# Blockwise-causal attention and a two-layer projection: longer ways to TensorE in the planner, another rule for the shared port, and a new table of priorities

## The chip, the core and the metric

The kernel runs on one core of a Trainium2 chip. Such a core has a matrix engine (TensorE, PE in the profile), a vector engine (VectorE, DVE), an activation engine (ScalarE, ACT), a general one (GpSimd, POOL) and SyncE (SP), from whose queue nearly all transfers between the chip's memory and the on-chip buffers are issued. Each engine takes its own list of instructions in order; they wait for one another by semaphores. TensorE writes into eight banks of an accumulation memory, from which ScalarE and VectorE read.

The metric is the device time of one execution in microseconds; less is better. The time before is the median of three runs.

## What is computed

Attention over 8 batches of 8 heads, 576 positions of 64 numbers, with a mask in blocks of 64 (a position sees its own block and the blocks before), and on its result, as 4608 rows of 512 numbers, two projections with an activation between them. All is fp32.

```python
scores = scale * np.matmul(q, k.transpose(0, 1, 3, 2))
mask = block_i >= block_j                      # block = position // 64
scores = np.where(mask, scores, -1000000000.0)
scores = scores - np.max(scores, axis=-1, keepdims=True)
attn = np.exp(scores)
attn = attn / (np.sum(attn, axis=-1, keepdims=True) + 1e-09)
out = np.matmul(attn, v)
...
x = np.ascontiguousarray(attn_out.transpose(0, 2, 1, 3)).reshape(B * S, H * D)
h = x @ w_in                                   # 512 -> 2048
g = np.maximum(h, 0.0) + alpha * np.minimum(h, 0.0)
return (g @ w_out).astype(np.float32)          # 2048 -> 512
```

## The kernel before

**Products in parts.** Most products are made from a rounded form of fp32 (fp32r in the rows). For that nearly every operand is split into a high part (a cast by ScalarE: gh, wa, X, w) and a low part (the difference, by GpSimd or VectorE: gl, xl), and a product is three: high by high, high by low, low by high. `split` (L552 the cast, L553 the difference) does this for most operands, `activate` (L677 to L686) for the activations of the first blocks. The weights come as 64-bit floats and are taken apart by `to_f32` (L529 to L546: one load, one step on ScalarE, five on VectorE, with two accumulation banks) before they are split.

**Stages.** (1) Attention goes by pairs of heads, 32 of them, and within a pair by tiles of 128 queries: scores (L1002 or L997, for the last 64 queries L1061 or L1067), maximum on VectorE (L1018, L1012, L1074), exponential on ScalarE (L1021, L1081), sum and reciprocal on VectorE (L1025, L1027), scaling on GpSimd (L1029, L1088), transposes on TensorE (L1037, L1094, L1103), copies of these to PTF and PT (L1112, L1114), and the product with the values (L1138). (2) Beside it, in chunks of 256 rows, the first 6 of the 16 blocks of the hidden dimension (`chunk_a`: L666 the first projection, L699 the second, L881 the partial result). They need nothing of the attention but its finished rows, and fill TensorE while the attention's chains run on the other engines. (3) When the attention is done, the other ten blocks follow in nine chunks of 512 rows, as five pairs of blocks by a scheme with seven products where plain 2 x 2 blocking has eight. `factors` loads 1 MB of x (xb) and makes the seven X. `pair1` makes the seven products of the first projection (L742, six multiplications of 128 x 256 each), which share three banks x, y, z. Between them ScalarE copies a bank (`keep`, L751) that a later product of the same pair adds onto; VectorE adds such a copy onto another bank (`onto`, L755) or to a sum (L773); `act` (L759 ScalarE, L760 VectorE) makes the activation c. `chunk2` makes the seven products of the second projection (L800), of which each runs over the five pairs, needs the high and low part of an activation (or of a sum of activations, L785) and 256 KB of weights w from memory (L793), and ends in L813 or L818, which put it onto the partial result.

**What sets the order.** Nothing in the code's order does. Each piece of work is entered by `op` with its engine, a cost in ns, what it reads and writes, the buffers that it claims and a priority (less is earlier). `SHIFTS` holds small numbers that are added to the priorities: the key is the priority itself, rounded. Then `Plan.schedule` plays the program through once, event by event: an engine that is free takes, of its pieces that are ready, the one with the least priority for which buffers are free. A piece is ready when what it depends on has ended, plus a way between the two engines from the table `LAT` (in ns). The order in which the pieces were taken is the order in which the instructions are issued, engine by engine. The reckoned times themselves go nowhere else: on the chip an instruction waits for its semaphores, be the reckoning right or wrong.

Two further rules touch the change. The planner lets VectorE and GpSimd share a port: it holds back any GpSimd piece, and any VectorE piece whose cost is of the kind `Port`, while the other one has it (`port`, the time until which it is taken). When both are free at the same moment, the engine with the lesser next priority is asked first. And TensorE's pieces cost more where the planner reckons with a slower clock (`clock`), from the columns streamed in the window before.

Of the kernel before, what the change touches and what calls it, by code (L numbers as in the profile page):

```python
# [142 lines left out]
class Plan:  # L143
# [45 lines left out]
    def schedule(self):  # L189
# [22 lines left out]
        for i in range(n):  # L212
            if not waits[i]:
                heapq.heappush(events, (0.0, 0, i))
        blocked = {}
        port = 0.0

        def wake(key):
            for x in blocked.pop(key, ()):
# [14 lines left out]
        while events:  # L234
            t = events[0][0]
# [12 lines left out]
            for engine in sorted(ready, key=lambda e: (e in ("DVE", "POOL"), ready[e][0] if ready[e] else (0, 0))):  # L248
# [16 lines left out]
                if chosen is None:  # L265
                    continue
# [1022 lines left out]
```

## Time and profile before

| what | value |
|---|---|
| median of 3 runs | 1094.94 us (1093.42 to 1095.65) |
| the profiled execution: device time | 1101.07 us |
| its span, first to last instruction | 1099.3 us |
| mean granted TensorE clock | 0.996 of full |
| DMA | 233.37 MB, mean 212 GB/s |
| of it through memory | 150.22 MB read, 37.49 MB written |

The profile is one execution, taken apart by instruction. Its page gives the busy time of each engine (weight loads of TensorE apart, as PEld); the trace answers the same for any stretch of time, what an engine waited for, and the instructions in order of time. Times in such rows are in us from the span's start. A row of a timeline has the start, the time until its last instruction ended, the engine, the line, the operation, what is written and read, the shape and the count, and in brackets the idle time before it with what ended it. Idle time under 0.15 us is not listed as a wait. A multiplication's end is modelled, so that products which follow each other closely look like one busy stretch, even where the starts are a little apart.

### The profile page before, as it was taken

To read this page: it belongs to the slowest core of one execution; us is meant where nothing else is said; L and a number is where in the kernel's file an instruction comes from. 1 tells how busy PE (TensorE), PEld (TensorE's weight loads), DVE (VectorE), ACT (ScalarE), POOL (GpSimd) and SP (SyncE) were. 2 spreads that over 40 slices of the span, in tenths; PEclk is the share of its full clock that TensorE was granted. 3 is DMA by queue.
4 is the path that set the end of the run, shared out by engine and by line. 5 is a ranking of instruction groups with operands and counts; after the bars stand their busy time and mean duration, and the time that the engine had idled before them with its cause. 6 is when DMAs were issued, how large, how long until landed. Compare 5 with 4: busy or idle time off the path is not lost. (4 is left out here: it accounts for less than half of the span.)

```text
span 1099.3 us, 24631 instructions
## 1 busy us (share of the span) xinstructions
PE 1076.1 (98%) x8158; PEld 971.6 (88%) x8158; DVE 754.4 (69%) x1703; ACT 702.4 (64%) x1969; POOL 711.9 (65%) x913
## 2 busy tenths in 40 slices
PE   7989999999999999999999999999999999999998
PEld 4667788888988889888889898999999999999998
DVE  7977675575576664756647778686776768586666
ACT  7878866676676676667655465656565656565553
POOL 4767657757667666576548866585767667675731
PEclk9999999999999999999999999999999999999999
DMA  6596885877568675866515365587877768686874
GB/s 199 187 273 194 241 253 146 245 207 228 151 197 258 192 212 182 233 210 193 143 48 202 102 221 182 176 277 217 271 229 255 256 223 286 200 297 195 298 254 156
DMA packets 139807, 233.37 MB, mean 212 GB/s; under 512 B 14880, under 2 KB 52256, under 8 KB 139680
## 3 DMA queue, kind: packets, MB, share of 16 engines
q1 hardware_dynamic: 138960, 231.15, 68.7%
q8 instruction: 65, 1.06, 0.4%
q10 hardware_dynamic: 720, 0.66, 0.2%
q14 instruction: 62, 0.51, 0.1%
HBM read 150.22 MB, written 37.49 MB: 171 GB/s over the span
## 5 line engine op out<-in xcount | busy, mean ns | idle before, releaser
L742 PE MATMUL bank<-X,w 128*128 128x256 f32 x1890 | 247.7, 286 | 1.7 <-ACT X L552 1.0
L742 PEld LDWEIGHTS bank<-X,w 128*128 128x128 f32 x1890 | 235.8, 190 | 3.9 <-ACT X L552 1.2
L800 PE MATMUL bank<-w,gh 128*128 128x256 f32 x1260 | 228.2, 281 | 1.8 <-ACT gh L552 1.7
L553 POOL TENSOR_TENSOR gl<-c,gh 128x256 fp32r<-128x256 f32 x177 | 153.7, 883 | 100.0 <-ACT gh L552 99.9
L1029 POOL TENSOR_SCALAR p<-p,ri 128x256 f32<-128x256 f32 (+3 forms) x256 | 138.0, 554 | 90.8 <-DVE ri L1027 53.8
L800 PEld LDWEIGHTS bank<-w,gh 128*128 128x128 f32 x1260 | 193.6, 189 | 2.6 <-ACT gh L552 2.6
L800 PE MATMUL bank<-w,gl 128*128 128x256 f32 x630 | 177.4, 282 | 1.6 <-POOL gl L553 1.6
L1021 ACT ACTIVATE p<-bank,nm 128x384 f32<-128x384 f32 (+3 forms) x256 | 134.3, 534 | 29.4 <-DVE nm L1018 15.3
L699 PE MATMUL bank<-wa,gh 128*128 128x512 f32 x432 | 139.1, 403 | 0.0
L666 PE MATMUL bank<-xh,wa 128*128 128x256 f32 x864 | 127.5, 286 | 2.4 <-ACT wa L552 1.5
L552 ACT CAST gh<-c 128x256 fp32r<-128x256 f32 x199 | 80.2, 407 | 64.1 <-PE bank L800 56.6
L800 PEld LDWEIGHTS bank<-w,gl 128*128 128x128 f32 x630 | 118.9, 189 | 2.4 <-POOL gl L553 2.4
L666 PEld LDWEIGHTS bank<-xh,wa 128*128 128x128 f32 x864 | 114.0, 191 | 6.9 <-ACT wa L552 1.7
L686 POOL TENSOR_TENSOR gl<-g,gh 128x256 fp32r<-128x256 f32 x108 | 83.6, 777 | 41.6 <-ACT gh L683 24.4
L1037 PE MATMUL bank<-ident,p 128*128 128x128 f32 x640 | 100.4, 281 | 6.7 <-POOL p L1029 5.9
L997 PE MATMUL bank<-K,Q 128*128 128x512 f32 (+1 forms) x448 | 93.9, 332 | 1.9 <-DMA K<-KL 1.2
L1138 PE MATMUL bank<-PTF,vraw 128*64 128x320 f32 (+3 forms) x768 | 94.8, 386 | 0.4 <-ACT p L1021 0.4
L1037 PEld LDWEIGHTS bank<-ident,p 128*128 128x128 f32 x640 | 75.0, 143 | 22.6 <-POOL p L1029 12.6
L679 DVE SCALAR_TENSOR_TENSOR g<-g,oal,bank 128x256 f32<-128x256 f32 x108 | 51.6, 478 | 62.4 <-ACT g L677 61.8
L1018 DVE TENSOR_REDUCE nm<-bank 128x1 f32<-128x512 f32 (+3 forms) x144 | 80.3, 586 | 17.4 <-PE bank L997 12.4
L553 POOL TENSOR_TENSOR gl<-raw,gh 128x256 fp32r<-128x256 f32 x74 | 64.5, 882 | 36.0 <-ACT gh L552 35.7
L751 ACT COPY g<-bank 128x256 f32<-128x256 f32 x135 | 50.1, 372 | 56.8 <-PE bank L742 56.7
(163 smaller groups left out, 2179.1 us busy)
## 6 DMA issues: line engine op xcount, KB each, us to landing
w<-wd SPq DMA_DIRECT2D x315, 256.0 KB, 4.3
Q<-QH SPq DMA_DIRECT2D x56, 256.0 KB, 3.8
K<-KH SPq DMA_DIRECT2D x112, 128.0 KB, 3.6
vraw<-in_v SPq DMA_DIRECT2D x32, 320.0 KB, 3.4
qraw<-in_q SPq DMA_DIRECT2D x30, 320.0 KB, 4.1
xd<-xT SPq DMA_DIRECT2D x8, 1152.0 KB, 7.2
part<-o SPq DMA_DIRECT2D x36, 256.0 KB, 3.0
xb<-xd SPq DMA_DIRECT2D x9, 1024.0 KB, 7.6
```

What stands on the lines that cost most here:

```text
L553: op(on, c_pool(n) if on == "POOL" else c_ss(n), lambda: (nc.gpsimd if on == "POOL" else nc.vector).tensor_tensor(out=lo(), in0=src(), in1 ...
L666: nc.tensor.matmul(hp()[:, :n], ww()[:, 0, cc * P:(cc + 1) * P], x()[:, cc, :n], start=(i == 0 and cc == 0), stop=(i == 2 and cc == NCC - 1))
L686: op("POOL", c_pool(CHA), lambda: nc.gpsimd.tensor_tensor(out=gl(), in0=g(), in1=gh().bitcast(F32), op=ALU.subtract), r=[g, gh], w=[gl], p ...
L699: nc.tensor.matmul(acc(), a()[:, ts], ww(), start=(first and i == 0), stop=(last and i == 2))
L742: nc.tensor.matmul(bank()[:, :CHA], W()[:, i, 256 * at + P * c:256 * at + P * c + P], B()[:, j, CHA * c:CHA * c + CHA], start=(first and n ...
L800: nc.tensor.matmul(bank()[:, CHA * i:CHA * i + CHA], a()[:, P * i:P * i + P], W()[:, x], start=(first and g + i + n == 0), stop=(g == NG - ...
L997: nc.tensor.matmul(o, Q()[:, i, qs], K()[:, 2 * h + i, :w], start=(i == 0), stop=(i == 1))
L1018: op("DVE", c_dve(w), lambda h=h: nc.vector.tensor_reduce(out=nm()[:, h:h + 1], in_=sb[h]()[:, off[h]:off[h] + w], axis=AX.X, op=ALU.max, ...
L1021: op("ACT", 238 + w / 1.2, lambda h=h, t=t: nc.scalar.activation(out=t()[:, :w], in_=sb[h]()[:, off[h]:off[h] + w], func=AF.Exp, bias=nm() ...
L1029: op("POOL", 244 + w / 1.2, lambda h=h: nc.gpsimd.tensor_scalar(out=pts[h]()[:, :w], in0=pts[h]()[:, :w], scalar1=ri()[:, h:h + 1], scalar ...
L1037: nc.tensor.transpose(out=tp()[:, base + c * P:base + (c + 1) * P], in_=pts[h]()[:, c * P:(c + 1) * P], identity=ident)
L1138: nc.tensor.matmul(ob()[rows[h], a - q0:q1 - q0], V()[:, c, h, :], moving, start=(c == 0), stop=(c == cs[-1][0]))
```

## The change

Three edits, all in the planner. The pieces of work, their costs and buffers and what they depend on are the same: 7430 pieces before and after.

First, the ways from ScalarE, VectorE and GpSimd to TensorE are reckoned as 255, 235 and 220 ns instead of 158, 135 and 118. Second, an engine of the two on the port notes the time since when it has been held back by it (`since`), and where both could go, the one that has waited longer is asked first. Third, `SHIFTS` has other numbers and many more: it reaches the priorities of 4094 pieces in another way than before. Of the table one line stands here.

```diff
-    -11: 1.5, -6: -0.5, -4.5: 1.3, -4: -3, -3.5: -6.1, 0: 2.2, 0.5: 0.1, 1: 2.7, 2: 3.4, 4.5: -1.2, 9: 2.6, 10: 1.7, 10.5: -0.8, 11: -0.8,
+    -11.75: -0.1, -11.5: 0.3, -10.5: -0.6, -9: 2.6, -8: -0.8, -7: 0.9, -5.5: -6.8, -4.5: 1.1, -4: -1.8, -3.5: -6.1, -3: 6.4, 0: 2.6,
...
-LAT = {("PE", "ACT"): 200, ("PE", "DVE"): 200, ("PE", "POOL"): 250, ("PE", "SP"): 250, ("ACT", "DVE"): 140, ("ACT", "PE"): 158,
-       ("ACT", "POOL"): 178, ("ACT", "ACT"): 110, ("ACT", "SP"): 180, ("DVE", "ACT"): 120, ("DVE", "PE"): 135, ("DVE", "POOL"): 235,
-       ("DVE", "DVE"): 115, ("DVE", "SP"): 150, ("POOL", "ACT"): 90, ("POOL", "DVE"): 90, ("POOL", "PE"): 118, ("POOL", "POOL"): 60,
+LAT = {("PE", "ACT"): 200, ("PE", "DVE"): 200, ("PE", "POOL"): 250, ("PE", "SP"): 250, ("ACT", "DVE"): 140, ("ACT", "PE"): 255,
+       ("ACT", "POOL"): 178, ("ACT", "ACT"): 110, ("ACT", "SP"): 180, ("DVE", "ACT"): 120, ("DVE", "PE"): 235, ("DVE", "POOL"): 235,
+       ("DVE", "DVE"): 115, ("DVE", "SP"): 150, ("POOL", "ACT"): 90, ("POOL", "DVE"): 90, ("POOL", "PE"): 220, ("POOL", "POOL"): 60,
...
-        port = 0.0
+        port, since = 0.0, {}
...
-            for engine in sorted(ready, key=lambda e: (e in ("DVE", "POOL"), ready[e][0] if ready[e] else (0, 0))):
+            for engine in sorted(ready, key=lambda e: (e in ("DVE", "POOL"), since.get(e, t), ready[e][0] if ready[e] else (0, 0))):
...
                 if chosen is None:
+                    if held:
+                        since.setdefault(engine, t)
                     continue
+                since.pop(engine, None)
```

What the planner makes of it is another order. Because the table is longer, a line of the kernel from the planner's end on has a number that is 73 higher after the change (L742 is L815, L800 is L873, L552 is L625, L785 is L858). Three places follow.

TensorE in stage 3, near 699 us of the profile before. First what stood there: five products of one pair of blocks at L742 without a break, of which the third and the fifth write the bank of the first (bank_144), with one product in between each time.

```order
L800 MATMUL bank_191<-w_7280,gl_552 128x256
L742 MATMUL bank_144<-X_7444,w_7272 128x256 x6
L742 MATMUL bank_183<-X_6662,w_7272 128x256 x6
L742 MATMUL bank_144<-X_6674,w_7272 128x256 x6
L742 MATMUL bank_174<-X_7247,w_7272 128x256 x6
L742 MATMUL bank_144<-X_6705,w_7272 128x256 x6
L800 MATMUL bank_191<-w_7292,gh_617 128x256 x2
```

And what stands there now, for the same pair of blocks (weights w_7272; its first bank is bank_181).

```order
L815 MATMUL bank_181<-X_7418,w_7272 128x256 x6
L815 MATMUL bank_144<-X_6668,w_7272 128x256 x6
L815 MATMUL bank_234<-X_7247,w_7272 128x256 x6
L815 MATMUL bank_181<-X_6675,w_7272 128x256 x6
L873 MATMUL bank_183<-w_7292,gh_676 128x256 x2
L873 MATMUL bank_183<-w_7292,gl_680 128x256
L873 MATMUL bank_183<-w_7292,gh_676 128x256 x2
L873 MATMUL bank_183<-w_7292,gl_680 128x256
L815 MATMUL bank_174<-X_7418,w_7267 128x256 x6
L815 MATMUL bank_181<-X_6719,w_7272 128x256 x6
```

The product that re-uses the first bank comes after two others, its next re-use after a product of the second projection and one of the next pair of blocks (w_7267).

ScalarE at the end of the first chunk of stage 3, near 677 us of the profile before. First the order before: gh are the high parts for the second projection, X_7251 the cast of a factor from a newly loaded xb.

```order
L552 CAST gh_695<-o_1264 128x256
L552 CAST X_7251<-xb_6596 128x512
L552 CAST gh_883<-c_7338 128x256
L552 CAST gh_990<-c_7405 128x256
L552 CAST gh_1179<-c_7493 128x256
L552 CAST gh_543<-c_7572 128x256
L552 CAST gh_617<-o_1264 128x256
L552 CAST gh_695<-c_7353 128x256
```

And now, from the same high part of o on.

```order
L625 CAST gh_761<-o_1216 128x256
L625 CAST gh_821<-c_7328 128x256
L625 CAST gh_973<-c_7416 128x256
L625 CAST gh_1117<-c_7505 128x256
L832 ACTIVATE g_6730<-bank_172 128x256
L625 CAST gh_588<-c_7577 128x256
L625 CAST gh_676<-o_1216 128x256
L625 CAST gh_761<-c_7338 128x256
L625 CAST gh_821<-c_7524 128x256
L625 CAST X_7251<-xb_6601 128x512
```

The cast of X has moved behind seven casts of gh that stood behind it.

ScalarE in the attention's start, near 70 us of the profile before: wa_948 is the high part of the fifth block's weights for the first projection, the p are exponentials of one pair's score tiles, m_252 the weights on their way through `to_f32`.

```order
L1021 ACTIVATE p_211,s_132<-bank_193,nm_203 128x512
L1021 ACTIVATE p_218,s_132<-bank_181,nm_203 128x512
L1021 ACTIVATE p_222,s_134<-bank_172,nm_209 128x384
L1021 ACTIVATE p_231,s_134<-bank_183,nm_209 128x384
L534 ACTIVATE bank_172<-m_252,ebias 128x512
L534 ACTIVATE bank_183<-m_327,ebias 128x512
L1142 COPY xT<-bank_193 128x320
L1021 ACTIVATE p_198,s_136<-bank_234,nm_261 128x256
L1021 ACTIVATE p_206,s_136<-bank_234,nm_261 128x256
L1114 COPY PT_108<-bank_191 64x128
L552 CAST wa_948<-m_252 128x512
```

Now the same weights (wa_880) come through before the exponentials p_211 and p_218 of that pair.

```order
L607 ACTIVATE bank_181<-m_252,ebias 128x512
L1187 COPY PTF_107<-bank_183 128x4x128
L1154 ACTIVATE pl_394,s_140<-bank_174,nm_261 128x288
L1154 ACTIVATE pl_394,s_140<-bank_193,nm_261 128x288
L1187 COPY PTF_107<-bank_191 128x4x128
L972 ACTIVATE QH_690<-qraw_200 128x640
L625 CAST wa_880<-m_252 128x512
L977 CAST KH_697<-kraw_189 128x576
L1094 ACTIVATE p_211,s_132<-bank_183,nm_203 128x512
```

The cast of the weights and the step of `to_f32` ahead of it (L534 before, L607 now) have moved past that pair's four large exponentials.

156 rows, old and new, of the table SHIFTS are left out of this document.

## The prediction

> **What bounds the kernel now.** I read the page's busy times first, then the same by stage, then what TensorE waited for, then the order of the instructions in time at the places where it waited.
>
> ```profile
> span 1099.3 us, 24631 instructions
> ...
> PE 1076.1 (98%) x8158; PEld 971.6 (88%) x8158; DVE 754.4 (69%) x1703; ACT 702.4 (64%) x1969; POOL 711.9 (65%) x913
> ```
>
> TensorE is busy for 98% of the span and no other engine for more than 69%. The change removes no instruction, so only two things can move the time: idle time of TensorE and the pace of its products. The busy time by stretches says where they are (two answers; the second number is the stretch's length, then busy time and count for PE, weight loads, DVE, ACT, POOL, then the granted clock):
>
> ```profile
> 20.00:60.00 40.00, 37.99 (x264) 25.28 (x266) 36.82 (x95) 33.07 (x92) 29.14 (x38) 1.00 0.61 185
> 60.00:100.00 40.00, 36.30 (x239) 28.63 (x238) 32.28 (x82) 32.56 (x93) 25.41 (x31) 0.96 0.81 234
> 100.00:141.00 41.00, 38.77 (x300) 32.34 (x301) 25.20 (x76) 34.99 (x112) 27.80 (x40) 1.00 0.89 244
> ```
>
> ```profile
> 300.00:400.00 100.00, 100.00 (x725) 84.93 (x723) 67.89 (x176) 71.04 (x216) 67.11 (x91) 1.00 0.75 210
> ...
> 600.00:660.00 60.00, 58.35 (x412) 54.10 (x411) 44.73 (x80) 35.53 (x87) 45.82 (x50) 1.00 0.48 159
> 660.00:700.00 40.00, 37.43 (x287) 35.82 (x286) 30.15 (x58) 21.76 (x60) 26.45 (x31) 0.96 0.53 169
> 700.00:800.00 100.00, 100.00 (x835) 99.71 (x835) 71.93 (x136) 58.12 (x153) 67.13 (x80) 1.00 0.77 246
> ```
>
> Four regimes follow. From 20 to 141 us TensorE idles 2.01 + 3.70 + 2.23 = 7.94 us while ScalarE works 33.07, 32.56 and 34.99 us of each stretch and VectorE 36.82 of the first 40: there the helpers nearly set the pace. In the middle (300 to 400) nothing idles. From 600 to 700 two seams cost 1.65 and 2.57 us. From 700 on the page shows a full TensorE; what is lost there can only be pace.
>
> **Part 1, the first projection's steady stage (640 to 1066 us).** The waiting that the page cannot show is in the starts of the products:
>
> ```profile
> 699.34 3.87 PE L742 MATMUL bank<-X,w 128*128 128x256 f32 x30
> 703.05 0.28 PE L800 MATMUL bank<-w,gh 128*128 128x256 f32 x1
> ```
>
> ```profile
> 705.19 0.41 PE L800 MATMUL bank<-w,gh 128*128 128x256 f32 x2
> ...
> 708.00 0.28 PE L742 MATMUL bank<-X,w 128*128 128x256 f32 x1
> ```
>
> ```profile
> 700.31 0.38 ACT L751 COPY g<-bank 128x256 f32<-128x256 f32 x1 [0.43 <-PE bank L742]
> ```
>
> Thirty multiplications at L742 take 703.05 - 699.34 = 3.71 us, 123.7 ns each; the four L800 products from 705.19 to 708.00 are 24 of the same shape in 2.81 us, 117.1 ns each. The five L742 products lose 3.71 - 30 x 0.1171 = 0.20 us. The order shown for this place says why: the third and the fifth write a bank that the first and the third wrote, and ScalarE's copy (L751) must have read it in between. The first product's own 6 x 0.117 = 0.70 us end near 700.04; the copy runs from 700.31 to 700.69; the third product should start two products in, at 699.34 + 2 x 0.70 = 700.74. Only 50 ns are left for the signal from ScalarE to TensorE. The planner before allows 422 ns from the copy's start to the product (a cost of 264 and a way of 158); 380 of copying leave 42 of them for the way. After, it allows 519. So each such re-use loses up to 0.20 / 2 = 0.10 us.
>
> Counted over the whole order, 135 of L742's 315 products re-use a bank that ScalarE copies; in 117 of them one product lies between in the order before, and in 4 after, where 90 have two and nearly all others more. With one more product of 0.70 us in between the wait is gone. The price: at most 113 x 0.10 = 11.3 us, at least nothing, were the loss L742's own pace. A second bound comes from the whole stage:
>
> ```profile
> 700.00:1066.00 366.00, 366.00 (x3052) 364.92 (x3052) 261.48 (x488) 211.08 (x556) 241.64 (x289) 1.00 0.77 249
> ```
>
> It runs 366.00 / 3052 = 119.9 ns a multiplication; at 117.1 it would save 8.5 us there and 9.9 from 640 on. That takes all of L742's slowness for waiting, and the group above was a bad one, so I take half of its price, 0.05 us: 113 x 0.05 = **5.6 us** (0 to 9.9).
>
> **Part 2, the seam at 660 to 700 us.** The timeline there:
>
> ```profile
> 674.76 0.19 PEld L800 LDWEIGHTS bank<-w,gl 128*128 128x128 f32 x1 [0.51 <-POOL gl L553]
> ...
> 678.75 0.62 ACT L552 CAST X<-xb 128x512 fp32r<-128x512 f32 x1 [1.53 <-DMA xb<-xd]
> 679.28 1.32 ACT L552 CAST gh<-c 128x256 fp32r<-128x256 f32 x4
> ...
> 679.73 0.51 PE L800 MATMUL bank<-w,gh 128*128 128x256 f32 x2 [0.91 <-ACT gh L552]
> ```
>
> ScalarE stands at a cast of X for a 1 MB load that has not landed, and the casts that TensorE needs now (gh) are queued behind it: 0.91 us. Ahead of that TensorE waits for GpSimd's low parts. In the new order seven gh casts stand before that X cast, and VectorE's sums for the last two products (L785 before, L858 now) stand four to six places earlier. So I take the whole idle time, 2.57 us (low end 0.9, the gh wait alone). The clock adds to it:
>
> ```profile
> 678.10:681.50 3.40, 1.99 (x12) 1.58 (x13) 2.06 (x4) 2.51 (x8) 1.75 (x2) 1.00 0.91 306
> 681.50:684.90 3.40, 3.40 (x18) 3.40 (x18) 1.82 (x3) 1.11 (x3) 3.40 (x5) 0.50 0.75 248
> 684.90:688.30 3.40, 3.40 (x30) 3.40 (x29) 1.78 (x5) 1.73 (x5) 2.16 (x3) 1.00 0.08 14
> ```
>
> After a window in which TensorE worked 1.99 of 3.40 us its granted clock is 0.50 for the next 3.40 us: 18 multiplications instead of 30, a loss of 12 x 0.117 = 1.4 us. If the window is filled this goes too; I take half of it, 0.7, since a rest of the idle may be enough to keep it. Together **3.2 us** (0.9 to 4.0). The Trainium skill, "TensorE: Matmul & The Clock Gate", section "Part 1: The HAM clock gate", gives the half clock to at least one idle window of some 3.4 us; by that rule stalls of 1 us cause none, the dip would stay and this part would be 2.57. The trace disagrees here, since the window ahead of the dip was 1.99 us busy.
>
> **Part 3, the attention's start (20 to 141 us).** TensorE's longest waits there:
>
> ```profile
> PE bank L666 <- ACT wa L552: 1.5, 1, 1.5
> PE bank L1103 <- POOL pl L1088: 1.3, 1, 1.3
> PE bank L997 <- DMA K<-KL: 1.2, 1, 1.2
> PE bank L1037 <- POOL p L1029: 1.1, 1, 1.1
> PE bank L666 <- POOL wa L553: 0.8, 2, 0.6
> ```
>
> The first, and the 0.6 us in the last, are one event: the low and high parts of the fifth block's weights (wa), which ScalarE casts late. In the new order that cast (wa) stands ten places earlier on ScalarE and the products that use it only three earlier on TensorE, so 1.5 + 0.6 = 2.1 us go. For the other three the order gives no clear answer; with ScalarE at 85% here, what is put first makes something else late. I leave them at nothing, and charge **1.0 us** for fresh waits, as 1815 of the 2278 pieces into which the planner cuts TensorE's work change places; the bounds are that all of the 7.94 us goes, and that it doubles. Net **1.1 us** (from 5.8 worse, 2.1 - 7.9, to 7.9 better).
>
> **What stays.** Ahead of the first seam and in the tail the rows around the waits are the same in both orders:
>
> ```profile
> PE bank L742 <- ACT X L552: 1.0, 1, 1.0
> PE bank L742 <- ACT g L751: 0.6, 1, 0.6
> ```
>
> ```profile
> 1088.25 0.47 PE L800 MATMUL bank<-w,gh 128*128 128x256 f32 x2 [0.83 <-ACT gh L552]
> ```
>
> The 1.6 us of 600 to 660 and the 0.83 at 1088.25 stay, and so do the first 35 products of TensorE, to about 25 us. The rule on the port costs nothing on the chip: it is the planner's, and what it changes is the place of VectorE's and GpSimd's instructions, which is in the parts above. No DMA is added. At the second seam the load of xb stands behind two more weight loads of 256 KB; the X cast that it feeds has moved back further, which hides it.
>
> **Sum.** 5.6 + 3.2 + 1.1 = 9.9 us, taken as 10. The profiled execution took 1101.07 us, 1.77 more than its span; less 10 it would take 1091. The median of the runs, 1094.94, lies 6.1 below the profiled one, so **1084.9 us**.
>
> **Rivals.** (a) The early gain is given back: ScalarE's 33.07 of 40 us is the limit, so part 3 is nothing, the dip of the clock stays and part 1 is half: 2.8 + 2.6 = 5.4, 1089.5 us. (By the Trainium skill's rule above the dip stays in every case.) For it speaks that L742 may be slower than L800 by itself; against it, that the loss sits at the re-uses. (b) More goes: half of the 7.94 us early, 4.0 at the seam, 6 in the steady stage: 14, 1080.9 us. (c) The change does not do what it says: the 123.7 ns are L742's own pace, and of the rest only the 0.9 us of the gh wait is saved: about 1094. (d) Slower, by the weight loads of the second projection. The new order sets L800 products earlier and more evenly among L742, each needs its own 256 KB w, and in the stretch 678.10 to 681.50 the DMA share was already 0.91 at 306 GB/s. If a w came 1.5 us late twice in each of the nine chunks, that is 27 us against the 10 gained, 1112 us; it decides from about 0.6 us per wait. Against it: over 700 to 1066 the share is 0.77, and nothing waits for w there now.
>
> **How the numbers follow.** The forecast has a chance of 0.55, (a) 0.20, (b) 0.10, (c) 0.08, (d) 0.07. The range reaches from just under (b) to between (a) and (c), 1080 to 1092, and leaves out (c), (d) and the edge of (b); the doubled early waits alone, 6.9 us worse than I take them, still end inside it at 1091.8. A difference of 0.2%, 2.2 us, is about what a measurement of this kernel can tell from none. Faster by more than that are the forecast, (a) and (b), 0.85; within it is (c), 0.08; slower is (d), 0.07.
>
> **What would show it.** Part 1 is right if the stretch from 700 to 1066 holds a multiplication every 118.5 ns or less, and wrong if it still needs 119.9. Part 2 is right if the seam near 675 us has under 1 us of TensorE idle and no granted clock of 0.50 after it. Part 3 is right if ScalarE's wa no longer is among TensorE's waits and the idle time from 20 to 141 us is below 7 us. The whole is wrong if a wait for w, or one for X, shows up on TensorE after 640 us.

## The result, and the profile after

| kernel | median us (lowest to highest, runs) | before, in the same measurement | ratio, 95% interval |
|---|---|---|---|
| after | 1085.97 (1084.34 to 1293.82, 7) | 1095.08 (7 runs) | 0.9907 [0.9882, 0.9933] |
| after, measured again | 1086.57 (1085.19 to 1088.45, 4) | 1097.27 (29 runs) | 0.9902 [0.9888, 0.9917] |

The change makes the kernel 9 to 11 us faster; 1084.9 was predicted, 1080 to 1092 as the range. Single runs far above all others, like the one at 1293.82 us here, are left out of the ratios and of the figures below.

The page of after, span and busy times:

```profile
span 1083.5 us, 24603 instructions
...
PE 1065.6 (98%) x8158; PEld 967.9 (89%) x8158; DVE 758.6 (70%) x1703; ACT 699.6 (65%) x1969; POOL 710.9 (66%) x913
```

The share of TensorE is the same 98% with 15.8 us less span: a share says nothing here, only the stretches do. These are the stretches of after that answer to those of before (start and end, length, then busy time and count of PE, weight loads, DVE, ACT, POOL, granted clock, DMA share, GB/s):

```profile
20.00:60.00 40.00, 38.21 (x264) 25.12 (x261) 36.54 (x96) 34.51 (x97) 28.62 (x38) 1.00 0.62 189
60.00:100.00 40.00, 37.48 (x252) 31.18 (x251) 31.37 (x76) 31.76 (x87) 27.60 (x35) 0.96 0.86 244
100.00:141.00 41.00, 40.71 (x317) 33.72 (x317) 28.50 (x84) 35.55 (x116) 25.87 (x38) 1.00 0.85 233
```

```profile
600.00:660.00 60.00, 57.12 (x401) 52.80 (x400) 46.25 (x85) 36.07 (x91) 45.08 (x49) 1.00 0.45 148
700.00:800.00 100.00, 100.00 (x846) 99.98 (x845) 73.13 (x136) 59.51 (x156) 68.51 (x83) 1.00 0.79 255
700.00:1066.00 366.00, 366.00 (x3092) 365.98 (x3091) 271.86 (x507) 214.76 (x562) 241.53 (x288) 1.00 0.78 254
```

```profile
660.00:700.00 40.00, 39.97 (x332) 39.29 (x331) 32.91 (x61) 22.60 (x62) 27.02 (x32) 1.00 0.65 212
```

From 20 to 141 us TensorE idles 4.60 us where it idled 7.94. From 600 to 660 it idles 2.88, more than the 1.65 before. The second seam is full and its clock is 1.00: 332 multiplications where 287 stood. From 700 to 1066 there are 3092 multiplications for 3052, 118.4 ns each for 119.9.

What TensorE waited for, in the whole of after (line, who released it: us in total, times, longest; the five largest, of which the first and the fourth lie in the first 20 us, as they did before):

```profile
PE bank L1110 <- POOL p L1102: 4.3, 2, 2.8
PE bank L1140 <- DVE g L752: 2.2, 1, 2.2
PE bank L873 <- POOL gl L626: 1.2, 1, 1.2
PE bank L584 <- DVE warm L481: 1.1, 1, 1.1
PE bank L815 <- ACT X L625: 1.0, 1, 1.0
```

The 1.5 us for ScalarE's wa are gone. The 1.0 us for X at the first seam stayed. Two are new: 1.2 us for a low part gl at 638.33 us, and 2.2 us in the attention's start, with a window of half clock behind it. The timeline of after and its windows there:

```profile
63.87 0.40 PE L1140 MATMUL bank<-KH,QH 128*128 128x288 f32 x1 [2.22 <-DVE g L752]
```

```profile
61.82:65.24 3.42, 1.37 (x11) 1.37 (x12) 3.09 (x6) 0.79 (x2) 0.74 (x1) 1.00 0.76 204
65.24:68.65 3.41, 3.41 (x13) 2.84 (x12) 3.32 (x8) 3.00 (x8) 1.28 (x1) 0.50 0.67 214
```

### The profile page after: what moved, and what is told of

It is laid out like the page before. It is cut to its first block, busy times and chain, and to the rows that moved or that the text cites. A ratio compares the mean times of both kernels' runs of the same rounds, so it can differ in the third digit from the quotient of the medians.

```text
span 1083.5 us, 24603 instructions
## 1 busy us (share of the span) xinstructions
PE 1065.6 (98%) x8158; PEld 967.9 (89%) x8158; DVE 758.6 (70%) x1703; ACT 699.6 (65%) x1969; POOL 710.9 (66%) x913
## 4 chain that ended last, share of the span: by engine, by line
PE 93%; DVE 3%; ACT 1%; POOL 1%; DMA 1%; issue 1%; DVEq 0%; POOLq 0%; ACTq 0%
PE bank L873 21%; PE bank L815 20%; PE bank L739 14%; PE bank L772 14%; PE bank L1211 8%; PE bank L1070 6%; PE bank L1110 6%; PE bank L1140 2%; PE bank L1167 1%; DMA raw<-in_w_in 1%; DVE nm L1091 1%; PE bank L1075 0%; POOL w L626 0%; DVE bank L609 0%; ACT p L1094 0%
## 5 line engine op out<-in xcount | busy, mean ns | idle before, releaser
L815 PE MATMUL bank<-X,w 128*128 128x256 f32 x1890 | 245.5, 282 | 1.7 <-ACT X L625 1.0
L815 PEld LDWEIGHTS bank<-X,w 128*128 128x128 f32 x1890 | 233.3, 189 | 2.6 <-ACT X L625 1.2
L873 PE MATMUL bank<-w,gh 128*128 128x256 f32 x1260 | 229.4, 281 | 0.8 <-ACT gh L625 0.8
L873 PEld LDWEIGHTS bank<-w,gh 128*128 128x128 f32 x1260 | 193.8, 189 | 1.0 <-ACT gh L625 1.0
L873 PE MATMUL bank<-w,gl 128*128 128x256 f32 x630 | 177.7, 282 | 1.2 <-POOL gl L626 1.2
L1094 ACT ACTIVATE p<-bank,nm 128x256 f32<-128x256 f32 (+3 forms) x256 | 134.5, 539 | 32.4 <-DVE nm L1085 16.3
L873 PEld LDWEIGHTS bank<-w,gl 128*128 128x128 f32 x630 | 118.9, 189 | 2.1 <-POOL gl L626 2.0
L1110 PE MATMUL bank<-ident,p 128*128 128x128 f32 x640 | 97.7, 279 | 4.9 <-POOL p L1102 4.3
L625 ACT CAST gh<-c 128x256 fp32r<-128x256 f32 x195 | 78.6, 407 | 36.8 <-PE bank L873 32.4
L832 ACT ACTIVATE g<-bank 128x256 f32<-128x256 f32 x135 | 50.8, 384 | 67.9 <-DVE bank L828 58.5
L1070 PE MATMUL bank<-K,Q 128*128 128x512 f32 (+1 forms) x448 | 89.7, 327 | 0.3 <-ACT pl L1154 0.3
L772 PEld LDWEIGHTS bank<-wa,gh 128*128 128x128 f32 x432 | 75.7, 190 | 13.9 <-issue 0.9
```

The lines of the kernel that those rows point to most:

```text
L772: nc.tensor.matmul(acc(), a()[:, ts], ww(), start=(first and i == 0), stop=(last and i == 2))
L815: nc.tensor.matmul(bank()[:, :CHA], W()[:, i, 256 * at + P * c:256 * at + P * c + P], B()[:, j, CHA * c:CHA * c + CHA], start=(first and n ...
L873: nc.tensor.matmul(bank()[:, CHA * i:CHA * i + CHA], a()[:, P * i:P * i + P], W()[:, x], start=(first and g + i + n == 0), stop=(g == NG - ...
L1070: nc.tensor.matmul(o, Q()[:, i, qs], K()[:, 2 * h + i, :w], start=(i == 0), stop=(i == 1))
L1094: op("ACT", 238 + w / 1.2, lambda h=h, t=t: nc.scalar.activation(out=t()[:, :w], in_=sb[h]()[:, off[h]:off[h] + w], func=AF.Exp, bias=nm() ...
L1110: nc.tensor.transpose(out=tp()[:, base + c * P:base + (c + 1) * P], in_=pts[h]()[:, c * P:(c + 1) * P], identity=ident)
```

## A table of three times that carries the experiments

TensorE's work is 2278 pieces in every version, and in every order piece 1649 is the first product of stage 3. From there on all pieces are products of six multiplications of one shape. So three times divide every trace in the same way, whatever the order: when the attention ends (the start of piece 1649), how long both seams take (from there to the start of piece 1711, some 50 us later), and the steady stage (from there to the start of the last piece). With them stand how many of L742's 135 re-uses of a copied bank have just one product in between, in the order, and how many windows of half clock fell into the seams.

| kernel | before stage 3 | in stage 3 | attention ends at us | seams us | half clocks in them | steady us | re-uses |
|---|---|---|---|---|---|---|---|
| before | old | old | 632.49 | 53.19 | 1 | 409.06 | 117 |
| before_again | old | old | 629.17 | 50.69 | 0 | 409.12 | 117 |
| stage3_only | old | new table, new ways | 629.52 | 52.52 | 2 | 404.31 | 3 |
| stage3_ways | old | new ways | 626.80 | 54.14 | 2 | 403.91 | 3 |
| attention_only | new table, new ways | old | 627.32 | 50.20 | 0 | 409.99 | 117 |
| att_ways | new ways | old | 625.86 | 54.47 | 1 | 409.24 | 118 |
| att_table | new table | old | 630.71 | 51.08 | 0 | 409.26 | 116 |
| stage3_old_ways | new table, new ways | new table | 623.87 | 54.69 | 2 | 407.63 | 84 |
| after | new table, new ways | new table, new ways | 625.37 | 49.40 | 0 | 404.21 | 4 |
| after_again | the same | the same | 626.09 | 49.40 | 0 | 404.17 | 4 |
| ways_only | new ways | new ways | 624.67 | 49.82 | 0 | 403.92 | 5 |
| table_only | new table | new table | 631.65 | 50.96 | 0 | 407.92 | 82 |
| act_way | ScalarE's way | ScalarE's way | 635.33 | 50.11 | 0 | 403.93 | 5 |
| fifth_x | new table, new ways | the same, more room for X | 625.90 | 52.11 | 1 | 404.49 | 3 |

Each row is one execution. In the steady column the two executions of before, and the two of after, agree within 0.1 us. But attention_only, whose order in stage 3 is that of before on every engine, needs 0.9 us more, so a difference under 1 us says little there. The first column spreads by 5.7 us over four executions of one order (632.49, 629.17, 629.52, 626.80), so there only groups can be compared: these four end at 629.5 us on the mean, the seven with the three new ways before stage 3 between 623.87 and 627.32, at 625.6 on the mean, and the two with the new table alone at 630.71 and 631.65.

Of the re-uses counted in the last column those that lie in the steady stage itself are 108 where the whole count is 116 to 118, 74 of the 84, 73 of the 82, and none in the other rows. The others lie in the seams.

## First experiments: which half of the program

The halves were cut apart at the first piece of stage 3: a table and ways for the pieces before it, others from it on. For the ways that is this edit (here the new ways in stage 3 alone, stage3_ways; attention_only, att_ways and stage3_old_ways have the old ones in LAT3 and the new ones in LAT); for the table, only those entries were exchanged that reach the half in question.

```diff
+LAT3 = {("ACT", "PE"): 255, ("DVE", "PE"): 235, ("POOL", "PE"): 220}
...
-                    ready_at[j] = max(ready_at[j], end + lat + LAT.get((engine, self.ops[j][0]), 0))
+                    ready_at[j] = max(ready_at[j], end + lat + ((LAT3 if j >= self.stage3 else {}).get((engine, self.ops[j][0])) or LAT.get((engine, self.ops[j][0]), 0)))
...
+    plan.stage3 = len(plan.ops)
     cs = first(0)
```

The kernel before once more, for a second profile:

> The kernel before, profiled a second time, because its first profiled execution (1101.07 us) took 6 us more than the median of its runs. If the first was an odd execution, this one takes about 1095 us and reaches stage 3 (the 1649th piece of TensorE, 632.49 us in the first) some 5 us earlier, with the steady stage after 700 us as before (119.9 ns a multiplication). If profiling itself costs 6 us, it takes 1101 again and stage 3 begins near 632.

The new table and ways in stage 3 alone:

> The order of before up to the end of the attention; in stage 3 the new table and the longer ways. Theory A (stage 3 carries the gain, as predicted: 5.6 us by the re-used banks and 3.2 at the seam): 1095.1 - 8.8 = 1086.3 us, 1085 to 1088, and no wait of TensorE over 0.5 us at the seam near 675 us. Theory B (the attention carries 7 us of the profile's difference): 1092 to 1094 us.

The new table and ways until stage 3 alone:

> The other half: the new table, ways and port rule up to the end of the attention, stage 3 planned as before. Theory A: 1.1 us less than before, 1094 us, 1092.5 to 1095.5. Theory B: 1088 us, as the profile of after reaches stage 3 7.1 us earlier than that of before.

The new ways, not the table, in stage 3 alone:

> Before, with the longer ways in stage 3 alone and the old table. 3 of the 135 re-uses of a bank have one product between them instead of 117, and the cast of X still stands before the seven casts of gh. Theory A (a re-use with one product between costs 0.05 us): 114 x 0.05 = 5.7 us less, 1089.4 us, with the seam's idle time as before; the stretch after 700 us at 118.5 ns a multiplication or less. Rival (the pace is L742's own): 1095 us and 119.9 ns.

| kernel | median us (runs) | ratio to before, 95% interval |
|---|---|---|
| before_again | 1095.29 (1) | span 1093.5 us, where the first profile's was 1099.3 |
| stage3_only | 1092.73 (5) | 0.9961 [0.9947, 0.9976] |
| attention_only | 1093.74 (12) | 0.9968 [0.9958, 0.9978] |
| stage3_ways | 1094.76 (12) | 0.9968 [0.9954, 0.9981] |

The second profile of before, at 1095.29 us, shows that profiling does not cost the 6 us. Over the 82 runs of before that were measured beside the experiments the median is 1096.9 us, from 1092.8 to 1101.6: the first profile, 1101.07 us, was one of the slowest executions, and the second one of the faster ones.

Both halves give something, and neither gives all. No theory came as written: stage3_only lies 4.3 us below before, where A asked for 8.8 and for no wait over 0.5 us at the second seam (it has one of 1.5 us for gh); attention_only lies 3.5 us below, where A asked for 1.1 and B for 7. (The bare times lie in B's range for the one and in A's for the other, but before took 1097.8 us in this measurement, not 1095.1.) The steady stage is settled by these: 366 us of it hold this many multiplications in before_again, in stage3_only and in stage3_ways:

```profile
684.00:1050.00 366.00, 366.00 (x3054) 364.93 (x3053) 261.84 (x487) 211.16 (x557) 243.75 (x291) 1.00 0.77 247
```

```profile
684.00:1050.00 366.00, 366.00 (x3091) 365.98 (x3091) 266.36 (x491) 215.46 (x564) 245.40 (x293) 1.00 0.76 249
```

```profile
684.00:1050.00 366.00, 366.00 (x3094) 366.00 (x3094) 269.73 (x492) 216.39 (x565) 249.26 (x293) 1.00 0.78 251
```

The ways alone do it, 409.1 to 403.9 us. That stage3_ways is nevertheless only 0.32% faster, 3.5 us where 5.7 were expected, fits its seams: 54.14 us, with two windows of half clock around a wait of TensorE for ScalarE's gh. ScalarE itself had been idle before that cast, for a sum of VectorE's (L786) and not for a load (two answers, TensorE and ScalarE):

```profile
672.71 0.80 PE L801 MATMUL bank<-w,gh 128*128 128x256 f32 x2 [1.72 <-ACT gh L553]
```

```profile
672.25 0.41 ACT L553 CAST gh<-c 128x256 fp32r<-128x256 f32 x1 [2.87 <-DVE c L786]
```

And before_again shows what the prediction could not know: its second seam has neither the half clock nor the 0.91 us for gh, with the very same order. TensorE idles 1.66 us there instead of 2.57, nearly all of it in four waits for gl.

```profile
660.00:700.00 40.00, 38.34 (x307) 36.87 (x306) 30.76 (x58) 20.83 (x58) 27.85 (x34) 1.00 0.58 189
```

The cast of X waits for its load there too, but the load lands about 1 us earlier against the work (678.75 in the first profile, where TensorE is 3.4 us later at that place; 674.43 here), in a gap of ScalarE's:

```profile
674.43 0.62 ACT L552 CAST X<-xb 128x512 fp32r<-128x512 f32 x1 [0.57 <-DMA xb<-xd]
```

## Second experiments: ways or table, half by half

The changed kernel once more, after_again:

> The changed kernel once more, for a second profile and a second set of times. If its gain has the places read so far (steady stage about 4.9 us, attention's start about 3.5, the seam at 660 to 700 the rest), the stretch from 684 to 1050 us holds 3085 multiplications or more, the seam idles less than 1 us without a half clock after it, and the time is 8 to 11 us below that of the kernel before on the same chip. If the profile of after was a lucky execution, the seam shows idle time or a half clock again, and the time is 5 to 7 us below.

The new table everywhere, the new ways until stage 3:

> The changed kernel with the old ways to TensorE in stage 3 alone. In its order 84 of L742's 135 re-uses of a copied bank have one product in between, where before has 117 and after has 4. If each such re-use costs 0.05 us, it keeps 33 x 0.05 = 1.65 us of the steady stage's gain: about 3065 multiplications from 684 to 1050 us (before 3050 to 3054, after 3092), and the time is about 4 us above after, more if the seam is late again, since the cast of X stands ahead of the gh casts there as before. If the table alone sets the pace of L742, the stretch holds 3085 or more, and the time is within 2 us of after.

The old table, the new ways until stage 3:

> The kernel before with the longer ways until stage 3 begins, the old table and the old ways in stage 3. Both changed until stage 3 gave 3.5 us (attention_only). If the ways give it, this run is 3 to 4 us faster than before and idles less than 5 us from 20 to 141 us (5.2 to 7.9 in four executions with the old order, 4.2 and 4.6 with the new); if the table gives it, it is within 1 us of before and idles 5 to 8 us. From 684 us on it is as before in both cases (3045 to 3054 multiplications to 1050 us).

The new table until stage 3, the old ways:

> The kernel before with the new numbers of the table that act until stage 3, and the old ways throughout. If the table gives the early gain, 3 to 4 us faster than before and less than 5 us idle from 20 to 141 us; if the ways give it, within 1 us of before. If the two only work together, since the numbers were found with the new ways, both this run and the last stay within 1 us of before, or are slower.

| kernel | median us (runs) | ratio to before, 95% interval |
|---|---|---|
| stage3_old_ways | 1094.14 (12) | 0.9976 [0.9965, 0.9988] |
| att_ways | 1095.48 (11) | 0.9984 [0.9975, 0.9993] |
| att_table | 1098.81 (12) | 1.0020 [1.0006, 1.0034] |

after_again came as the first case of its expectation says: 1086.57 us (in the table of the result), 10.7 below before, with the second seam full as in after.

stage3_old_ways is the dose between: 84 re-uses instead of 117 or 4, and its stretch holds 3066 multiplications, where 3065 were expected.

```profile
684.00:1050.00 366.00, 366.00 (x3066) 365.14 (x3065) 263.74 (x489) 213.07 (x558) 239.25 (x290) 1.00 0.75 247
```

In the steady stage 108, 74 and no such re-uses stand beside 409.1, 407.6 and 404.2 us: (409.1 - 404.2) / 108 = 0.045 us for each, and 34 of them make 1.5 us, as measured. (The 0.043 us in an expectation below come of dividing by 113, with those in the seams.) Its time, 7.6 us above after where about 4 were expected, has the rest in the seams again: 54.69 us in the traced execution, 5.3 more than after.

In the attention the ways count too: by the groups above it ends 3.9 us earlier with them, and no earlier with the table alone. att_table is the one kernel here that is slower than before, by 0.2%. Neither of the two expectations for att_ways was right as a whole, though: it is 1.8 us faster, not 3 to 4. In the traced execution what the attention gained is lost at the second seam, in one wait and the half clock behind it (timeline, then windows, of att_ways):

```profile
673.55 0.50 PE L801 MATMUL bank<-w,gh 128*128 128x256 f32 x2 [2.38 <-ACT gh L553]
```

```profile
671.34:674.76 3.42, 0.62 (x3) 0.42 (x4) 3.42 (x7) 1.67 (x6) 1.36 (x3) 1.00 0.88 328
674.76:678.17 3.41, 3.41 (x17) 3.41 (x18) 2.28 (x4) 1.08 (x3) 3.41 (x5) 0.50 0.33 82
```

My theory then was: the ways give the attention's gain and the steady stage's, and the table is what keeps the seams full. The next runs took it apart.

## Third experiments: the ways alone, the table alone, and a try at the first seam

Of the change's three edits, ways_only has the one on the ways and nothing else:

```diff
...
-       ("ACT", "POOL"): 178, ("ACT", "ACT"): 110, ("ACT", "SP"): 180, ("DVE", "ACT"): 120, ("DVE", "PE"): 135, ("DVE", "POOL"): 235,
+       ("ACT", "POOL"): 178, ("ACT", "ACT"): 110, ("ACT", "SP"): 180, ("DVE", "ACT"): 120, ("DVE", "PE"): 235, ("DVE", "POOL"): 235,
...
```

> The kernel before with the longer ways everywhere and the old table. By the parts measured so far the ways give 3.6 us in the attention (att_ways) and 4.9 in the steady stage (5 re-uses with one product in between), 8.5 in all. If the table matters at the seam alone, the steady stretch holds 3085 multiplications or more, the stretch from the first product of stage 3 to the end of the second seam (TensorE's pieces 1648 to 1710) takes 51 us or more where after takes 49.4, with a half clock likely, and the time is 2 to 5 us above after, 5 to 9 below before. If the table is needed everywhere, the time is within 3 us of before. If it is not needed at all, within 1 us of after.

And table_only has the one on the table:

```diff
 SHIFTS = {
-    -11: 1.5, -6: -0.5, -4.5: 1.3, -4: -3, -3.5: -6.1, 0: 2.2, 0.5: 0.1, 1: 2.7, 2: 3.4, 4.5: -1.2, 9: 2.6, 10: 1.7, 10.5: -0.8, 11: -0.8,
+    -11.75: -0.1, -11.5: 0.3, -10.5: -0.6, -9: 2.6, -8: -0.8, -7: 0.9, -5.5: -6.8, -4.5: 1.1, -4: -1.8, -3.5: -6.1, -3: 6.4, 0: 2.6,
...
```

> The kernel before with the whole new table and the old ways. 82 re-uses with one product in between: at 0.043 us each the steady stage gains 35 x 0.043 = 1.5 us, about 3065 multiplications from 684 to 1050 us. The attention is as in att_table, 1 us slower than before. So within 2 us of before, if the parts add up; 4 us or more below it if the table carries a gain of its own at the seams.

The third had this edit on top of after:

```diff
-        rooms("wb", ("w1", 3, [2, 7 * 256], F32R), ("w2", 4, [2, 256], F32R), ("xb", 1, [NCC, CHB], F32), ("X", 4, [2, 512], F32R),
-              ("m", 2, [512], F32), ("ws", 1, [512], F32), ("xt", 2, [512], F32), ("g", 4, [CHA], F32), ("c", 12, [CHA], F32))
+        rooms("wb", ("w1", 3, [2, 7 * 256], F32R), ("w2", 4, [2, 256], F32R), ("xb", 1, [NCC, CHB], F32), ("X", 5, [2, 512], F32R),
+              ("m", 2, [512], F32), ("ws", 1, [512], F32), ("xt", 2, [512], F32), ("g", 4, [CHA], F32), ("c", 8, [CHA], F32))
...
-        rooms("fx", ("w1", 2, [2, 7 * 256], F32R), ("w2", W2N, [2, 256], F32R), ("X", 4, [2, 512], F32R), ("c", CN, [CHA], F32))
+        rooms("fx", ("w1", 2, [2, 7 * 256], F32R), ("w2", W2N, [2, 256], F32R), ("X", 3, [2, 512], F32R), ("c", CN + 4, [CHA], F32))
```

> The changed kernel with the memory of stage 3's beginning shared out otherwise: 5 instead of 4 buffers for X from the attention's end on, and 8 instead of 12 for c until the first blocks' memory is free, the rest of both after that. In the order only 57 of TensorE's pieces move, all from the first seam on. If the 1.03 us in which TensorE waits there for X is the fifth X's wait for memory, the idle time from 600 to 640 us falls from 2.88 to about 2.2 us or less, and the time is 0.5 to 1 us below after, too little for the times alone. If the wait only moves to the sixth X, the idle time stays between 2.6 and 3 us and the time as after's. If the second seam is disturbed, it idles over 1 us there and loses 2 us or more.

| kernel | median us (runs) | ratio to before, 95% interval |
|---|---|---|
| ways_only | 1085.16 (4) | 0.9879 [0.9865, 0.9892] |
| table_only | 1097.68 (11) | 1.0001 [0.9987, 1.0015] |
| fifth_x | 1088.94 (5) | 0.9914 [0.9900, 0.9927] |

**The theory on the table fell.** With the three ways and the old table the kernel is at least as fast as with all of the change (0.9879 beside 0.9902 and 0.9907; the intervals overlap, so not shown to be faster). Its second seam is full:

```profile
660.00:700.00 40.00, 39.70 (x334) 39.29 (x333) 29.77 (x56) 22.56 (x62) 28.54 (x35) 1.00 0.71 231
```

And the table without the ways is worth nothing that can be measured, as its expectation has it if the parts add up. The steady stage of the traced execution gains 1.2 us where 1.5 were reckoned, and its attention ends at 631.65 us, 2.2 later than the mean of the old order but within that order's spread.

fifth_x did what it was to do at the first seam and gained nothing by it. TensorE idles 1.12 us from 600 to 640 instead of 2.88, and the wait for X is gone; but in the second seam of the traced execution, full in after, ScalarE's gh comes late and a half clock follows. Nor is it shown to be slower than after: the intervals, 0.9900 to 0.9927 and 0.9888 to 0.9917, overlap.

```profile
600.00:640.00 40.00, 38.88 (x254) 35.17 (x253) 32.10 (x55) 22.52 (x53) 29.96 (x34) 1.00 0.52 178
660.00:700.00 40.00, 37.68 (x300) 36.96 (x299) 30.38 (x58) 20.75 (x55) 24.03 (x29) 0.96 0.60 192
```

```profile
670.01 0.51 PE L874 MATMUL bank<-w,gh 128*128 128x256 f32 x2 [1.75 <-ACT gh L626]
```

## Last experiment: one number

The planner itself shows that ScalarE's way decides the re-uses, and that it has a step: with 230 ns, and the other two ways as before, 114 re-uses have one product in between, with 240 there are 106, with 255 there are 5. It reckons 200 ns from TensorE to ScalarE and 264 for the copy; with 255 for the way back that is 719, and a product is reckoned as 712 (6 x 117.3 x 1.012). Just above it, a second product has to go in between.

```diff
-LAT = {("PE", "ACT"): 200, ("PE", "DVE"): 200, ("PE", "POOL"): 250, ("PE", "SP"): 250, ("ACT", "DVE"): 140, ("ACT", "PE"): 158,
+LAT = {("PE", "ACT"): 200, ("PE", "DVE"): 200, ("PE", "POOL"): 250, ("PE", "SP"): 250, ("ACT", "DVE"): 140, ("ACT", "PE"): 255,
```

> The kernel before with one number changed: the way from ScalarE to TensorE is reckoned as 255 ns instead of 158. In its order 5 re-uses of a bank have one product in between and 127 have two. If the steady stage needs this number alone, the stretch from 684 to 1050 us holds 3085 multiplications or more (4.9 us). In the attention the high parts come from ScalarE, but most waits on GpSimd, so the theory leaves 1 to 3 of the 3.6 us that the three ways together gave there. The seam is open: 49.4 to 54.7 us from the first product of stage 3 to the end of the second seam, with the seven orders so far. Together 1086 to 1091 us where before takes 1097, and as ways_only (12 us below before) if the one number does it all. If VectorE's and GpSimd's ways carry the gain, the stretch stays under 3060 and the time within 2 us of before.

It took 1094.37 us (12 runs), 0.9984 [0.9974, 0.9993], above the 1086 to 1091 that were expected. The steady stage has all of its gain, 403.93 us, and the seams are good, 50.11. But in the traced execution the attention ends at 635.3, 5.8 us later than the mean of the old order and 2.8 later than the latest of its four: the weights are late again, by more (waits of act_way from 20 to 155 us, and its busy times):

```profile
PE bank L699 <- ACT wa L552: 2.8, 1, 2.8
PE bank L1094 <- ACT p L1021: 1.3, 1, 1.3
...
PE bank L699 <- POOL wa L553: 0.9, 1, 0.9
```

```profile
60.00:100.00 40.00, 32.78 (x186) 25.56 (x185) 27.55 (x70) 26.87 (x75) 23.56 (x30) 0.83 0.75 216
```

A clock of 0.83 over 40 us is four windows of half clock (40 x 0.17 x 2 = 13.6 us, 3.41 each). So VectorE's and GpSimd's ways are not needed for the steady stage. In the attention the three ways together gain and ScalarE's alone does not; which of the other two is needed there, and by what waits, was not tested.

## Why the prediction was right, and which steps were not

The sum was 9.9 us. Against before_again (1095.29 us) the trace of after gives 629.17 - 625.37 = 3.8 in the attention, 50.69 - 49.40 = 1.3 at the seams and 409.12 - 404.21 = 4.9 in the steady stage: 10.0. Against the first profile, from which the terms had been read, the same places give 7.1, 3.8 and 4.9. So the total was right, but of its three terms only the first had its size. The second was taken 1.9 us too high and the third 2.7 too low, measured from before_again, and that these two nearly cancel was luck.

- **Part 1, the re-uses (5.6): right, mechanism and size.** From piece 1711 on 108 re-uses are gone and with them 4.9 us, 0.045 us each where 0.05 was taken; the other 5 lie in the seams, where they can't be told from the rest. stage3_ways and act_way, in which the steady stage has the old table and the three ways or ScalarE's alone, show 5.1 to 5.2 us; stage3_old_ways loses what the line gives (1.5 us), table_only a little less (1.2 for 1.6). Rival (c), L742 slow by itself, is out: between 700 and 1060 us its 251 products took 732 ns on the mean from start to next start before, and its 248 took 712 after, where L800's take 708 and 709. So L742's own slowness is 3 or 4 of those 24 ns, and the rest was waiting.
- **Part 2, the second seam (3.2): the rows came as predicted, the price holds for one execution only.** After has no idle time there, and no half clock. But of the 3.8 us that separate the first profile from after's at the seams, 2.5 belonged to that one execution: with the same order before_again needed 2.5 us less. The step that failed is "I take the whole idle time" together with the half clock: the 0.91 us for gh hung on a load's landing, which came about 1 us earlier against the work in the second execution, and without that wait no half clock followed. The new wait of 1.2 us at the first seam then took a part of the gain back. Nor is it the place of X's cast that settles it. att_table has five of the seven gh casts ahead of it, attention_only none of them, and the seams of both are free of half clocks; stage3_only has six ahead, and two half clocks. In the five other traces with a half clock at the second seam (stage3_only, stage3_ways, att_ways, stage3_old_ways, fifth_x) the late cast of gh does not stand behind a cast of X that waits for a load: ScalarE is idle just before it, 0.88 to 3.83 us, for a sum of VectorE's.
- **Part 3, the attention's start (1.1): too low.** The wa wait went, as predicted, and fresh waits came too: the 2.22 us at 63.87 in after, none above 1.2 us in after_again. The listed idle time from 20 to 141 us fell from 6.25 us in before_again to 4.60 and 4.32 in the two executions of after, by 1.7 and 1.9. The step that failed is that this idle time was taken for all there is to win: stage 3 begins 3.8 and 3.1 us earlier, so 2.1 and 1.2 us of the gain are not in it. Where these lie, in half clocks, in idle time after 141 us or in pauses too short to be listed, was not taken apart. Idle from 20 to 141 us being below 7 us, which I had named as the sign, is no sign: before_again has 6.25.
- **What stays: half right.** Both waits of the first seam and the 0.8 us of the tail stayed. A third came at the first seam, the 1.2 us for gl at 638.33: in after a product of L800 starts at 636.74 us, where before ran L742 alone from 637.82 to 645.20.
- **The port rule: wrong as told.** I wrote that it changes the places of VectorE's and GpSimd's instructions. It changes none: as the planner gives it, the kernel before with this rule alone has, on every engine, the order of before, and after without it the order of after.
- **The half clock.** The prediction set a rule of the Trainium skill ("TensorE: Matmul & The Clock Gate", section "Part 1: The HAM clock gate"), by which the dip would stay, beside a window that was 1.99 us busy; the runs side with the window (last section).
- **Rivals.** (d) did not come: nothing waits for w on TensorE, with the DMA share at 0.78. (a), which gave the early gain back and halved the steady one, and (b), with 14 us, did not come either.
- **The reference execution.** I added the terms on a profile of 1101 us and then went down by the 6.1 us to the median. That offset wasn't spread evenly: the two profiles of before differ by 3.3 us until stage 3 and 2.5 at the seams, the very places that two terms were read from.

What stays open: why some orders keep the seams full, and by which waits the three ways shorten the attention. The eight traces without a half clock at the seams need 49.4 to 51.1 us there, the six with one or two need 52.1 to 54.7; no count of the order that I tried tells them apart beforehand. At most there is a tendency: of the six traces in which the cast of X stands ahead of all seven gh casts, as in before, four have a half clock at the second seam, of the eight with four to seven of them ahead of it two.

How often an order falls into a half clock can be read for the whole kernel, not for the seams: every run has its mean granted clock, and (1 - clock) x 2 x time is an estimate of the time at half clock, to about 1 us in a single run. It is 6.3 us a run over 82 runs of before and 2.6 over ten of after. Of the others ways_only and attention_only have 3.8, table_only and att_table 4.8, att_ways 6.2, stage3_only 7.4, stage3_old_ways 10.8, act_way 11.7 and stage3_ways 13.3. So after has less half clock than before on the mean of its runs; by the same estimate that is worth at most half of the 3.7 us between them, 1.9 us. fifth_x, with 2.2 us over five runs, has no more of it than after, so the half clock of its trace is not typical.

## What to carry to other kernels

Where a scheduler reckons with a latency, look for the step that it decides (here: does copy and way fit under one product or not), and take the time from the starts of the instructions, not from the busy share. Before a large table is blamed or praised, run the small edits alone: three numbers gave at least as much as all of this change. And take a second profile before terms are read from waits that hang on a transfer.

## What had not been expected of the hardware

The granted clock is set for windows of 3.41 us, and a half clock needs no idle window. In each of the 14 traces the stretches at half clock begin on one grid of 3.41 us and, ahead of the tail, last one or two of its steps. From 18 us on the traces hold some 4300 windows of that grid at full clock. All ten in which TensorE was busy for less than 0.53 of the time were followed by one at half clock, and none of those above 0.59 was; in between it was six of eleven. The prediction's window, 1.99 of 3.40 us busy (0.585), is one of the six. Two that were followed by a full clock, 0.60 busy in before and 0.56 busy in att_table:

```profile
633.73:637.14 3.41, 2.04 (x15) 1.63 (x14) 0.91 (x2) 1.41 (x5) 0.00 (x0) 1.00 0.86 272
637.14:640.56 3.42, 3.20 (x25) 2.95 (x25) 2.53 (x5) 3.42 (x9) 1.61 (x2) 1.00 0.89 280
```

```profile
641.00:644.42 3.42, 1.92 (x16) 1.81 (x16) 1.81 (x4) 1.81 (x5) 3.42 (x6) 1.00 1.05 400
644.42:647.83 3.41, 3.41 (x31) 3.41 (x30) 2.74 (x5) 1.86 (x7) 3.25 (x4) 1.00 0.78 263
```

(Busy is counted by the rows, with their modelled ends.) So, as an estimate, 1.5 us of waiting cost 1.5 us if they are split over two windows, and some 3 us if they fall into one: by the prediction's rows a half clock takes 12 multiplications, 1.4 us. The seams column agrees: without a half clock none is above 51.1 us, with one none is below 52.1.
